# A recurrence and a token mixer as one hand-ordered program: another order of its steps, another queue for the last store

## The chip, the cores and the metric

The kernel runs on one core of a Trainium2 chip. The metric is device time in microseconds (us), given as the median of some runs. Five engines work from their own instruction lists: TensorE (PE, matmuls), VectorE (DVE), ScalarE (ACT), GpSimd (POOL) and SyncE (SP), which here issues nearly all the DMA transfers. An engine runs its list in the order in which it is written, and an instruction that waits for another engine holds up all that stand behind it.

## The reference

```python
f = sigmoid(f_logit)                                   # B=4, H=8, S=768, D=48
for t in range(S):                                     # first part: a gated recurrence
    state = f[:, :, t, :, None] * state + k[:, :, t] (outer) v[:, :, t]
    y[:, :, t] = q[:, :, t] @ state
x = y as (B, S, H * D)                                 # 4 x 768 x 384
theta = x @ w_theta                                    # second part
zr, zi = x * cos(theta), x * sin(theta)
u = x + w_tok_r @ zr + w_tok_i @ zi                    # mixes the 768 tokens
out = u + relu(u @ w_ch)                               # mixes the 384 channels
```

All inputs and the output are fp32.

## The kernel before

The recurrence runs in chunks of 128 tokens, 24 of them (4 batches of 6), each in two halves of 64. The second part runs per chunk up to the rotated z, and then in 8 groups (batch and half of the output tokens).

The program is one flat list of 1166 two-letter steps, `ORDER` (L53 to L89). Each letter pair is a function (L554 to L568), called with a running number of its own: the ninth `th` is chunk 8's angles. A suffix `/A`, `/D` or `/P` runs that step on ScalarE, VectorE or GpSimd in place of its usual engine; an `h` in front means one half of chunk 0. Every engine's list is the steps in this order (`manual_schedule`, L517), so the string alone sets who is ahead of whom on every engine and in the queues of transfers. The steps that matter below:

- **Loads** by SP: `lf`, `lk`, `lq` (a chunk's gate, k and q, 256 KB; L524), `lv` (v, 288 KB; L529), `lw` (a part of a weight, two transfers of 384 KB, tile `raw`; L178).
- **Gate:** `go` (exponential and logarithm, ScalarE, L237), `gs` (a running sum, VectorE, L242), `ge` (two exponentials, ScalarE: tiles `p` and `f`, L249), `gp` (copy of the last column of `p`, GpSimd, L253), `gq` (q times p, L257; on GpSimd with `/P`), `gk` (k times f, L262).
- **Recurrence of chunk m:** `ke` (transposes k, TensorE, L321), `kt` (copies them out, `ktok`, of which there is one buffer), `sc` (scores: v with ktok, L295, and q with k, L301), `sa`, `st`, `sm` (VectorE: middle state L330, new state L336, its fade L340, this one sometimes on GpSimd), `ma` (mask, L307), `oa` and `ob` (q with the states, L354; v with the masked scores, L365), `xc` (the copy of the result out of PSUM, tile `x`, L372), `xt` (transposes, L377), `xs` (a copy that is kept, tile `ut`).
- **Second part:** `xh`, `xl` (splitting x into two parts), `th` (angles, L407), `tn`, `se`, `ab` (the angle brought into range: L412, L418, L423), `tr` (two sines on ScalarE, L430, with a table load when the table changes), `ro` (z, L438), `zh`, `zl` (splitting z), `f` (a piece of the token products, L461, six matmuls; 144 pieces), `v`, `uh`, `ul` (u and its split), `c` (channel product, L479), `cv` (relu and sum, L493), `so` (a store, L500).
- **Weights:** `d2` (ScalarE reads the upper halves, L193, tile `top`), `d3` (VectorE joins the bits, L197), `d4`, `d5`, `e4`, `e5` (the split into two parts, L207 to L216).
- `wu` is a matmul whose result nobody reads (L316). `fl` and `rv` test whether the gates stayed in range; where they didn't, a slow path behind `tc.If` (L626) does all of it again.

Two pools of PSUM set much of the pacing. Bank "a" (4 buffers) holds scores, transposes and angles; "mix" (4) holds the products. Scores take two "a" banks per chunk, which are given back when `xc` has copied the result out. The last group's three stores go on ScalarE's queue: two in `store` (L499) and the third behind the slow path (L658).

Of the kernel before, what the change touches and what calls it, by code (L numbers as in the profile page):

```python
# [20 lines left out]
B, H, S, D = 4, 8, 768, 48  # L21
DM = H * D
P = 128
# [5 lines left out]
TH = 384  # L29
# [59 lines left out]
)  # L89


@with_exitstack
def gla_moe_kernel(
    ctx: ExitStack,
    tc: tile.TileContext,
    q: bass.AP,
    k: bass.AP,
    f: bass.AP,
    v: bass.AP,
# [605 lines left out]
```

## Time and profile before

| | us |
|---|---|
| median of 3 runs | 334.79 (334.3 to 336.13) |
| the profiled execution | 333.83 |
| its span, first to last instruction | 332.0 |
| TensorE busy | 319.2 (96%) |
| VectorE busy | 249.0 (75%) |
| ScalarE busy | 198.1 (60%) |
| GpSimd busy | 49.3 (15%) |

TensorE's granted clock is 0.999 of full speed over the span. The shares are means over very different stages, so the rows below give them by stretch. In the rows, L12 is line 12 of the kernel, `out<-in` are tiles by their names in the program, x is a count, and `ACTq` or `SPq` is the engine's list where it issues transfers. In chains and waits a name like "ACT x L146" stands for the instruction that was waited for.

### The profile page before, as it was taken

To read this page: it belongs to the slowest core of one execution; us is meant where nothing else is said; L and a number is where in the kernel's file an instruction comes from. 1 tells how busy PE (TensorE), PEld (TensorE's weight loads), DVE (VectorE), ACT (ScalarE), POOL (GpSimd) and SP (SyncE) were. 2 spreads that over 40 slices of the span, in tenths; PEclk is the share of its full clock that TensorE was granted. 3 is DMA by queue.
4 is the path that set the end of the run, shared out by engine and by line. 5 is a ranking of instruction groups with operands and counts; after the bars stand their busy time and mean duration, and the time that the engine had idled before them with its cause. 6 is when DMAs were issued, how large, how long until landed. Compare 5 with 4: busy or idle time off the path is not lost.

```text
span 332.0 us, 10297 instructions
## 1 busy us (share of the span) xinstructions
PE 319.2 (96%) x4430; PEld 295.3 (89%) x4430; DVE 249.0 (75%) x451; ACT 198.1 (60%) x361; POOL 49.3 (15%) x65
## 2 busy tenths in 40 slices
PE   7689999999998999999999999999999999999994
PEld 7578777668998999999999999999999999999993
DVE  3799999999997999898954686766687868533252
ACT  6789999995988978474765487526854024300000
POOL 3411123114234220012100220200010100000000
PEclk9999999999999999999999999999999999999999
DMA  7989998456543170253035134108101000000022
GB/s 213 351 264 318 348 328 325 143 190 251 193 148 101 36 232 36 67 190 115 24 113 196 43 129 138 57 2 265 46 2 38 28 24 26 0 24 26 24 73 76
DMA packets 22080, 43.16 MB, mean 130 GB/s; under 512 B 2448, under 2 KB 6288, under 8 KB 22032
## 3 DMA queue, kind: packets, MB, share of 16 engines
q1 hardware_dynamic: 21600, 41.88, 38.0%
q8 instruction: 36, 0.59, 0.7%
q10 hardware_dynamic: 432, 0.59, 0.5%
q14 instruction: 12, 0.10, 0.1%
HBM read 37.74 MB, written 4.72 MB: 128 GB/s over the span
## 4 chain that ended last, share of the span: by engine, by line
PE 85%; DVE 4%; DMA 4%; ACT 3%; SPq 1%; issue 1%; DVEq 0%; ACTq 0%
PE pm L461 43%; PE pch L479 12%; PE pth L407 11%; PE pss L365 4%; PE pss L354 4%; PE pss L295 3%; PE pss L301 3%; PE psk L321 3%; PE pxt L377 2%; DMA raw<-in_w_theta_dram 2%; DMA raw<-in_w_i_dram 2%; SPq L524 1%; DVE k L262 1%; ACT z L146 1%; ACT top L193 1%
## 5 line engine op out<-in xcount | busy, mean ns | idle before, releaser
L461 PE MATMUL pm<-wp,z 128*128 128x384 f32 x756 | 144.4, 340 | 0.0
L461 PEld LDWEIGHTS pm<-wp,z 128*128 128x128 f32 x756 | 130.1, 188 | 1.2 <-DVE wp L216 0.3
L479 PE MATMUL pch<-uhl,wch 128*128 128x384 f32 x216 | 41.4, 340 | 0.0
L479 PEld LDWEIGHTS pch<-uhl,wch 128*128 128x128 f32 x216 | 37.2, 188 | 0.2
L242 DVE TENSOR_TENSOR_SCAN f<-carry,f 128x512 f32<-128x512 f32 (+1 forms) x25 | 29.2, 1173 | 4.0 <-ACT f L238 3.9
L407 PE MATMUL pth<-wth,xh 128*128 128x384 f32 x144 | 30.1, 344 | 0.9 <-ACT x L146 0.9
L146 ACT CAST uhl<-ut 128x384 fp32r<-128x384 f32 x12 | 6.2, 516 | 38.0 <-DVE uhl L146 19.9
L493 DVE SCALAR_TENSOR_TENSOR ut<-pch,ut 128x384 f32<-128x384 f32 x24 | 13.1, 553 | 20.6 <-PE pch L479 20.6
L407 PEld LDWEIGHTS pth<-wth,xh 128*128 128x128 f32 x144 | 24.7, 188 | 1.7 <-ACT x L146 1.2
L461 PE MATMUL pm<-value,zf 128*128 128x384 f32 x72 | 26.0, 497 | 0.0
L307 DVE TENSOR_TENSOR sc<-pss,causal 128x256 f32<-128x256 f32 x48 | 18.0, 415 | 7.3 <-PE pss L354 7.1
L257 POOL TENSOR_TENSOR q<-q,p 128x512 f32<-128x512 f32 x13 | 17.2, 1323 | 41.0 <-ACT p L249 39.3
L340 POOL TENSOR_TENSOR st<-st,pes 128x192 f32<-128x192 f32 x12 | 8.7, 721 | 94.0 <-DVE st L336 94.0
L249 ACT ACTIVATE p<-f 128x512 f32<-128x512 f32 (+1 forms) x25 | 15.2, 609 | 9.8 <-DVE f L242 9.0
L253 POOL COPY pes<-p 128x4 f32<-128x4 f32 x24 | 11.4, 475 | 64.9 <-ACT p L249 64.9
L438 DVE TENSOR_TENSOR w<-w,x 128x768 f32<-128x768 f32 x18 | 17.4, 967 | 3.0 <-ACT w L431 2.9
L262 DVE SCALAR_TENSOR_TENSOR k<-f,k 128x512 f32<-128x512 f32 (+1 forms) x25 | 18.4, 740 | 1.2 <-ACT f L250 1.2
L146 ACT COPY x<-pss 128x192 f32<-128x192 f32 x34 | 9.1, 318 | 17.2 <-PE pss L365 17.1
L461 PEld LDWEIGHTS pm<-value,zf 128*128 128x128 f32 x72 | 12.8, 189 | 7.0 <-DVE zf L438 0.4
L365 PEld LDWEIGHTS pss<-v,sc 64*64 64x64 f32 x768 | 15.9, 134 | 3.1 <-issue 0.8
L365 PE MATMUL pss<-v,sc 64*64 64x48 f32 x768 | 18.4, 222 | 0.0
L295 PE MATMUL pss<-v,ktok 64*64 64x48 f32 x704 | 16.4, 220 | 1.7 <-DMA v<-in_v_dram 1.2
(86 smaller groups left out, 573.3 us busy)
## 6 DMA issues: line engine op xcount, KB each, us to landing
v<-in_v_dram SPq DMA_DIRECT2D x24, 288.0 KB, 3.8
f<-in_f_dram SPq DMA_DIRECT2D x23, 256.0 KB, 3.7
k<-in_k_dram SPq DMA_DIRECT2D x23, 256.0 KB, 4.1
q<-in_q_dram SPq DMA_DIRECT2D x23, 256.0 KB, 4.1
raw<-in_w_r_dram SPq DMA_DIRECT2D x12, 383.8 KB, 5.1
raw<-in_w_i_dram SPq DMA_DIRECT2D x12, 383.8 KB, 5.7
out_dram<-ut SPq DMA_DIRECT2D x21, 192.0 KB, 2.4
raw<-in_w_theta_dram SPq DMA_DIRECT2D x3, 383.8 KB, 6.3
```

The lines of the kernel that those rows point to most:

```text
L146: (nc.scalar.copy if on(usual) is nc.scalar else on(usual).tensor_copy)(dst, src)
L242: nc.vector.tensor_tensor_scan(fl, carry[:, pairs(h)].rearrange("p n t -> p (n t)"), fl, 0.0, ALU.mult, ALU.add)
L249: nc.scalar.activation(ps_[m][:, pairs(h)], ft, AF.Exp, scale=-1.0)
L257: on(nc.vector).tensor_tensor(qt, qt, ps_[m][:, pairs(h)], op=ALU.mult)
L262: nc.vector.scalar_tensor_tensor(kt, loaded["f", m][:, pairs(h)], E_TOP, kt, op0=ALU.min, op1=ALU.mult)
L295: nc.tensor.matmul(pkvs[m][t][r, p, :], kts[m][ts, p, r], vs[m][ts, h * D:(h + 1) * D], start=True, stop=True)
L307: masked = nc.vector.tensor_tensor(scs[m][j], pss[m][j][:, :, :64], causal.unsqueeze(1).to_broadcast([P, NP, 64]), op=ALU.mult)
L365: nc.tensor.matmul(pys[m][j][ts, p, :], l, r, start=(old[t] is None and p == 0), stop=(p == NP - 1))
L407: nc.tensor.matmul(pths[m], l, r, start=(n == 0), stop=(n == len(ms) - 1))
L438: nc.vector.tensor_tensor(zfs[m] if full else w, w, xs[m].unsqueeze(1).to_broadcast([P, 2, DM]), op=ALU.mult)
L461: nc.tensor.matmul(pms[g, d], l, r, start=(s == 0 and i == 0), stop=(s == NC - 1 and i == len(ms) - 1))
L479: nc.tensor.matmul(pcs[g, d], l, r, start=(es[0] == 0 and n == 0), stop=(es[-1] == KD - 1 and n == len(ms) - 1))
```

## The change

Three edits, of which the first is nearly all:

1. `ORDER` is replaced by another order of the same steps. The running numbers keep their meaning; what changes is where a step stands, and on which engine some of them run. Of the steps with a choice of engine, VectorE gets fewer `tn` (11 to 4) and `kt` (9 to 7), more `uh` (12 to 16), `xh` and `xc` (7 to 9 each); GpSimd gets chunk 0's `gq` halves and two more `d5`; ScalarE has 24 table loads where it had 26.
2. Chunk 0's q is loaded whole: one transfer of 256 KB, not two of 128 KB.
3. The last store goes through `store` to SP's queue, ahead of the slow path's branch; the line behind the slow path is gone. SP gets a branch hint as the other engines have.

```diff
 ORDER = (
-    "wu wu wu wu wu hlf hlq wu hlf hgo lf hgo lf hlq hlk hlk hgs hgs wu go hge hge go lk wu wu wu lw wu wu",
+    "wu wu hlf hlf wu hgo hgo hgs hlq hgs lf hge hge wu wu lf hgq/P hlk wu hgk wu wu hlk lw lk wu wu hgk lv",
...
-    "uh so so c ul cv v uh cv c bh rv ul f so cv so v uh/D ul c c c cv so cv so so cv",
+    "so cv so f f fl f f f ul f c v v c uh/D bh rv ul c uh/D cv so ul c cv so cv so cv so",
 )
...
     def store(b, g, d):
         th = g % NTH
-        queue = nc.scalar if g == B * NTH - 1 and not general else nc.sync
+        queue = nc.scalar if g == B * NTH - 1 and d < 2 and not general else nc.sync
         queue.dma_start(out[b, d * P:(d + 1) * P, th * TH:(th + 1) * TH], uts[g][:, d, :])
...
     fn = {"h" + s: lambda n, go=go: go(n // 2, n % 2) for s, go in by_halves.items()}
+    fn["hlq"] = by_halves["lq"]
...
-    fn["bh"] = lambda _: tc.mark_branch_hint_location("general", engines=[nc.tensor.engine, nc.vector.engine, nc.scalar.engine])
+    fn["bh"] = lambda _: tc.mark_branch_hint_location("general", engines=[nc.tensor.engine, nc.vector.engine, nc.scalar.engine, nc.sync.engine])
...
-    nc.scalar.dma_start(out[B - 1, 2 * P:, (NTH - 1) * TH:], uts[LAST][:, 2, :])
```

What the string moves shows best on the engines' own lists, at the places where TensorE waits. The number behind a letter is the chunk or part, the one behind `_` only a tile's serial number, and it differs between the two programs.

SP's transfers at the start, before (`raw0` is the first part of w_theta, `raw1` its rest):

```order
L524 DMA f0_102<-in_f_dram 128x256
L524 DMA q0_104<-in_q_dram 128x256
L524 DMA f0_102<-in_f_dram 128x256
L524 DMA f1_111<-in_f_dram 128x512
L524 DMA f2_115<-in_f_dram 128x512
L524 DMA q0_104<-in_q_dram 128x256
L524 DMA k0_118<-in_k_dram 128x256 x2
L524 DMA k1_133<-in_k_dram 128x512
L178 DMA raw0_138<-in_w_theta_dram 128x1535 x2
L524 DMA q1_155<-in_q_dram 128x512
L529 DMA v0_157<-in_v_dram 128x576
L529 DMA v1_164<-in_v_dram 128x576
```

and after:

```order
L701 BRANCH_PREFETCH_HINT
L524 DMA f0_99<-in_f_dram 128x256 x2
L524 DMA q0_109<-in_q_dram 128x512
L524 DMA f1_112<-in_f_dram 128x512
L524 DMA f2_121<-in_f_dram 128x512
L524 DMA k0_124<-in_k_dram 128x256 x2
L178 DMA raw0_131<-in_w_theta_dram 128x1535 x2
L524 DMA k1_134<-in_k_dram 128x512
L529 DMA v0_139<-in_v_dram 128x576
L524 DMA q1_142<-in_q_dram 128x512
L529 DMA v1_153<-in_v_dram 128x576
L524 DMA q2_172<-in_q_dram 128x512
```

The hint is new at the head, q0 is one row, w_theta stands ahead of k1, and v0 ahead of q1.

VectorE's list at the start, before, from the running sum of chunk 2 to chunk 1's new state:

```order
L242 SCALAR_TENSOR_TENSOR f2_115<-carry_67,f2_115 128x512
L262 SCALAR_TENSOR_TENSOR k1_133<-f1_111,k1_133 128x512
L197 SCALAR_TENSOR_TENSOR raw0_138<-raw0_138,top0_88 128x768
L330 COPY mid0_233<-pss00_199 128x192
L336 TENSOR_TENSOR st0_269<-pss01_200,mid0_233 128x192
L340 TENSOR_TENSOR st0_269<-st0_269,pes_82 128x192
L332 TENSOR_TENSOR mid1_280<-pss10_235,st0_269 128x192
L336 TENSOR_TENSOR st1_282<-pss11_236,mid1_280 128x192
```

and after:

```order
L242 SCALAR_TENSOR_TENSOR f2_121<-carry_67,f2_121 128x512
L262 SCALAR_TENSOR_TENSOR k1_134<-f1_112,k1_134 128x512
L197 SCALAR_TENSOR_TENSOR raw0_131<-raw0_131,top0_88 128x768
L257 TENSOR_TENSOR q1_142<-q1_142,p1_166 128x512
L330 COPY mid0_242<-pss00_198 128x192
L336 TENSOR_TENSOR st0_244<-pss01_199,mid0_242 128x192
L340 TENSOR_TENSOR st0_244<-st0_244,pes_82 128x192
L332 TENSOR_TENSOR mid1_282<-pss10_248,st0_244 128x192
L336 TENSOR_TENSOR st1_284<-pss11_249,mid1_282 128x192
```

The multiplication of q1 (L257), GpSimd's before, now stands here between the joining of w_theta's bits (L197) and chunk 0's middle state (L330).

ScalarE's list between the copy of chunk 10's keys and that of chunk 9's result, before:

```order
L146 COPY ktok10_1630<-psk10_1587 128x512
L430 ACT_TABLE_LOAD
L430 ACTIVATE w6_1340<-w6_1340 128x384
L431 ACTIVATE w6_1340<-w6_1340,pair_79 128x384
L430 ACTIVATE w7_1566<-w7_1566 128x384
L431 ACTIVATE w7_1566<-w7_1566,pair_79 128x384
L146 CAST z6_1693<-w6_1340 128x768
L146 CAST wp14_1695<-value4_731 128x768
L146 CAST wch1_87<-raw15_1580 128x384
L146 COPY x9_1723<-pss90_1438 128x4x48
L146 COPY x9_1723<-pss91_1439 128x4x48
```

and after:

```order
L146 COPY ktok10_1600<-psk10_1567 128x512
L146 COPY ut2_1205<-pxt8_1544 128x3x128
L146 CAST wch1_87<-raw14_1428 128x768
L193 CAST top0_88<-raw15_1558 128x384
L225 ACT_TABLE_LOAD
L249 ACTIVATE p12_1687<-f12_1310 128x512
L250 ACTIVATE f12_1310<-f12_1310 128x512
L146 CAST wp12_1707<-value2_408 128x768
L146 COPY x9_1717<-pss90_1436 128x4x48
L146 COPY x9_1717<-pss91_1437 128x4x48
```

The sines of w6 and w7 and the split of z6 (L146, `z6`) no longer stand between them; the gate of chunk 12 (L249, L250) with its table does.

TensorE's list at the angles of chunk 8, before:

```order
L461 MATMUL pm12_1363<-wp113_1523,z5_1574 128x384
L461 MATMUL pm12_1363<-wp013_1606,z5_1574 128x384
L461 MATMUL pm12_1363<-wp113_1523,z5_1574 128x384 x2
L461 MATMUL pm12_1363<-wp013_1606,z5_1574 128x384
L461 MATMUL pm12_1363<-wp113_1523,z5_1574 128x384
L407 MATMUL pth8_1749<-wth1_85,xh8_1584 128x384 x3
L407 MATMUL pth8_1749<-wth0_84,xh8_1584 128x384 x3
L407 MATMUL pth8_1749<-wth1_85,xl8_1624 128x384 x3
```

and after:

```order
L461 MATMUL pm11_1347<-wp113_1525,z5_1575 128x384
L461 MATMUL pm11_1347<-wp013_1614,z5_1575 128x384
L461 MATMUL pm11_1347<-wp113_1525,z5_1575 128x384 x2
L461 MATMUL pm11_1347<-wp013_1614,z5_1575 128x384
L461 MATMUL pm11_1347<-wp113_1525,z5_1575 128x384
L321 MATMUL psk11_1723<-ident_74,k11_1224 128x128 x4
L407 MATMUL pth8_1730<-wth1_85,xh8_1625 128x384 x3
L407 MATMUL pth8_1730<-wth0_84,xh8_1625 128x384 x3
L407 MATMUL pth8_1730<-wth1_85,xl8_1679 128x384 x3
```

One product piece that stood ahead of the angles has moved away (`pm12`, behind this place now), and the transposes of k11 stand ahead of them.

## Rows read from the trace of the kernel before

**Rows 1.** busy us of each engine by stretch (x instructions), granted clock, DMA share, GB/s

```profile
16.00:33.00 17.00, 15.07 (x382) 13.47 (x375) 16.43 (x31) 15.78 (x34) 3.20 (x4) 1.00 0.88 285
33.00:72.00 39.00, 39.00 (x631) 28.06 (x630) 38.13 (x66) 37.66 (x68) 7.76 (x9) 1.00 0.76 270
72.00:107.00 35.00, 34.10 (x510) 31.18 (x508) 33.03 (x53) 28.05 (x51) 13.59 (x10) 1.00 0.56 180
107.00:327.00 220.00, 219.76 (x2755) 212.28 (x2755) 152.03 (x287) 105.32 (x188) 19.20 (x27) 1.00 0.23 74
```

**Rows 2.** TensorE's waits: engine, line, waited for, us in total, times, longest

```profile
PE pss L295 <- DMA v<-in_v_dram: 1.2, 1, 1.2
PE pth L407 <- ACT x L146: 0.9, 1, 0.9
PE pss L295 <- ACT ktok L146: 0.5, 2, 0.3
```

**Rows 3.** the chain of waits, first 36 us: start us, us, what

```profile
5.53 6.68 DMA raw<-in_w_theta_dram
...
13.43 1.62 DVE raw L197
...
15.89 1.47 DVE st L340
...
17.46 0.37 DVE mid L332
...
34.26 2.05 PE pm L461 x6
```

**Rows 4.** timeline of ScalarE: start, us, instruction, [idle before <- releaser]

```profile
14.55 0.59 ACT L146 COPY ktok<-psk 128x512 f32<-128x512 f32 x1 [1.21 <-PE pss L295]
```

**Rows 5.** timeline of ScalarE, 84 to 110 us

```profile
88.45 0.52 ACT L146 COPY x<-pss 128x192 f32<-128x192 f32 x2
...
91.77 0.49 ACT L412 ACTIVATE w<-pth 128x384 f32<-128x384 f32 x1 [1.08 <-PE pth L407]
93.14 0.48 ACT L146 CAST xh<-pxt 128x384 fp32r<-128x384 f32 x1 [0.89 <-PE pxt L377]
...
104.95 0.84 ACT L146 CAST z<-w 128x768 fp32r<-128x768 f32 x1 [1.43 <-DVE w L438]
...
106.86 0.53 ACT L146 COPY x<-pss 128x192 f32<-128x192 f32 x2
```

**Rows 6.** timeline of TensorE, 100 to 110 us

```profile
102.22 0.78 PE L365 MATMUL pss<-v,sc 64*64 64x48 f32 x32
...
107.22 1.32 PE L407 MATMUL pth<-wth,xh 128*128 128x384 f32 x6 [0.90 <-ACT x L146]
```

**Rows 7.** timeline of GpSimd, 0 to 62 us

```profile
15.87 1.27 POOL L257 TENSOR_TENSOR q<-q,p 128x512 f32<-128x512 f32 x1
...
43.39 1.26 POOL L340 TENSOR_TENSOR st<-st,pes 128x192 f32<-128x192 f32 x1 [4.06 <-DVE st L336]
```

**Rows 8.** timeline of VectorE, 9 to 34 us

```profile
29.51 0.35 DVE L340 TENSOR_TENSOR st<-st,pes 128x192 f32<-128x192 f32 x1
...
32.24 0.95 DVE L197 SCALAR_TENSOR_TENSOR value<-raw,top 128x768 int32<-128x768 int32 x1
```

**Rows 9.** timeline of VectorE, the last 7 us

```profile
326.14 1.60 DVE L493 SCALAR_TENSOR_TENSOR ut<-pch,ut 128x384 f32<-128x384 f32 x3 [2.09 <-PE pch L479]
```

**Rows 10.** the output's stores from 327 to 328.3 us: ns min/median/max, starts, landing

```profile
L500 ACTq DMA_DIRECT2D out_dram<-ut x2: 386/706/1027, 326.7 to 327.2; - x2
...
DMA to landing us min/median/max: 2.5/2.7/3.0
```

**Rows 11.** the output's stores from 328.5 to 330 us

```profile
L658 ACTq DMA_DIRECT2D out_dram<-ut x1: 432/432/432, 328.7 to 328.7; - x1
...
DMA to landing us min/median/max: 2.0/2.0/2.0
```

**Rows 12.** the page's DMA issues: count, KB each, median us to landing

```profile
out_dram<-ut SPq DMA_DIRECT2D x21, 192.0 KB, 2.4
```

66 rows, old and new, of the table ORDER are left out of this document.

## The prediction

> **What bounds the kernel now.** I read the stretches first, because a share over the whole span mixes stages. In [rows 1] the reader is to see four stages. From 16 to 33 us ScalarE is busy for 15.78 of 17 us and VectorE for 16.43 of 17, while TensorE has holes. From 33 to 72 us TensorE is busy for all 39.00 us, and VectorE (38.13) and ScalarE (37.66) run almost as full beside it. From 72 to 107 TensorE has its only larger hole after the start. From 107 to 327 us TensorE is busy for 219.76 of 220 us with the other engines far below it. So from about 34 us on the span is TensorE's own work, and that work is the same 1166 steps before and after, less one transfer. An order can gain in three places only: before 34 us, in the hole near 106 us, and behind TensorE's last matmul at 327 us.
>
> The list of TensorE's waits comes next [rows 2]: 1.2 us for chunk 0's v, 0.9 us before an angle product (L407) for the copy of x, and 0.5 us for ktok. Then the chain of waits of the first 34 us [rows 3] shows what the start hangs on: the transfer of w_theta (issued 5.53, landed 12.21), its joining on VectorE (13.43, 1.62 us), the fade of chunk 0's state (15.89, 1.47 us), chunk 1's middle state (17.46), and at last the first product, f0, at 34.26.
>
> **The head.** The new order of SP's transfers sends k1 behind w_theta and q1 behind v0. Each is 256 KB. With the transfers at 0.88 of their time the next stretch moved 285 GB/s [rows 1]; at that rate 256 KB are 0.9 us, and I count 0.7, since several transfers share the queue. So w_theta lands near 11.5 us and v0 about 0.7 us sooner too, which is inside the 1.2 us that the first scores wait for v [rows 2]. What pays for it is k1, which lands near 12; VectorE's step on k1 stands ahead of the joining of w_theta, and its end at about 12.7 us is still level with ScalarE's conversion that the joining needs. q1 is now VectorE's, behind the joining, and takes a slot there that GpSimd had.
>
> The joining itself took 1.62 us beside a GpSimd multiplication of q; the same operation on the same shape takes 0.95 us alone [rows 3, 7, 8]. GpSimd's q1 is gone from that moment (its q0 halves are early), so −0.67. The fade took 1.47 us beside GpSimd's q2 (15.87 to 17.14) against 0.35 us alone [rows 3, 7, 8]. In the new order q2 needs an exponential that now stands behind a 0.9 us conversion of w_theta on ScalarE, so the fade at about 15.5 us is over before q2 starts near 16: −1.1. Against these stands q1 on VectorE, +0.7 at most, beside the wait for the scores.
>
> Walking the new order with these durations, chunk 0's scores start at about 13.1 instead of 13.8, ktok of chunk 1 near 13.9 instead of 14.55 [rows 4], and chunk 1's middle state near 15.9 instead of 17.46: the chain leads by 0.7 to 1.6 us. It can't all arrive: from 16 us ScalarE has only 17 − 15.78 = 1.22 us of idle time up to the first sines [rows 1], and in the new order the conversions of w_theta and chunk 3's gate stand ahead of x0. Bounds for f0: 0 (ScalarE eats all) and −1.6. I take **−0.9**: the 0.7 us with which ktok leads, and a little of ScalarE's slack. Loading q0 whole costs nothing there, since it is read only after chunk 0's exponentials.
>
> **The hole at 106 us.** [Rows 6] show the angle product of chunk 8 starting at 107.22, after 0.90 us of nothing. It waits for a PSUM bank: the "a" banks are four, and the one it needs is emptied by the copy of x9 on ScalarE. That copy ran at 106.86 behind z6, wp14 and wch1, and z6 had made ScalarE wait 1.43 us for VectorE [rows 5]; the attention matmuls that x9 reads were done at 103.0 [rows 6].
>
> In the new order I count ScalarE's rows from x8 to x9: by the durations of this trace they are about 17.2 us before and 15.8 after (out go tn7, xh8, z6 and wp14, all with their waits; in come w6's and w7's absolute values, z5 and the gate of chunk 12). Before, x8 ran at 88.45 and x9 18.41 us later, of which 1.08 + 0.89 + 1.43 = 3.40 us were waits for work that is no longer there [rows 5]. So x9 comes 18.41 − 3.40 − 1.4 = 13.6 us after x8. x8 itself can't be earlier than TensorE gives it: the attention of chunk 8 now stands one product piece (f23, about 1 us) further back, at 89.5: x9 near 103.1, or at once after the attention of chunk 9 at about 104. TensorE wants the bank after f34, now for the transposes of k11, one product piece earlier than before and so near 105.0. The cover is about half a us once x9 is copied; the two pairs of sines in front are what can use it up. I take **−1.0**: the 0.90 us and a tenth, since matmuls overlap at their ends. Its bounds are −1.1 and, if ScalarE is as late as it is today while TensorE wants the bank one piece earlier, +0.9.
>
> **The rest between 34 and 327 us.** ScalarE has two table loads less and VectorE some 4 us less work, GpSimd about 4 us more; under a full TensorE that is worth nothing. The two waits for ktok make 0.5 us together [rows 2]. The new order puts about 3.4 us more of ScalarE's work ahead of ktok9 and only 1.0 us more of TensorE's, so that one stays, and I allow for two more of its size and for SP's added branch hint: **+0.4**. Bounds: −0.7 (all of [rows 2]'s ktok waits and the 0.24 us of 107 to 327 go) and the rival below.
>
> **The tail.** VectorE's last operation ends at 327.74 [rows 9]. Before, the last of three stores was issued only behind the branch, at 328.7, and landed 2.0 us later, at 330.7 [rows 11]. The two ahead of it were issued at 326.7 and 327.2 and landed after up to 3.0 us, so at 330.2 [rows 10]. Now SP issues the last one at about 327.8, and SP's stores land after 2.4 us [rows 12]: 330.2 as well. So **−0.5**, no more, because the second store is late next. Bounds 0 (the end waits for something else) and −0.9 (the 328.7 to 327.8 in full).
>
> **Sum.** −0.9 − 1.0 + 0.4 − 0.5 = −2.0. The profiled execution took 333.83 us (span 332.0 and 1.83 around it): 331.8. The median of the runs, 334.79, lies 0.96 above that execution, so I predict 332.8. About 0.5%, 1.7 us, is what a measurement of this kernel tells from no change.
>
> **Rivals.**
> *The gains come back as other waits.* A lead at 34 us is kept only if no operand is late after it, and VectorE and ScalarE are within 1 or 2 us of full up to 72 us [rows 1]. If they eat the head's lead and the hole at 106 moves to another bank or ktok, only the tail is left: 333.83 − 0.5 + 0.96 = 334.3. For it: every wait of TensorE here has a ScalarE or VectorE copy behind it. Against it: VectorE's load falls.
>
> *GpSimd holds up VectorE between 33 and 72 us (slower).* The new order hands GpSimd q4, q6 and the fade of chunk 2 in or before this stretch. Where the two engines met, each lost: GpSimd's fade of chunk 4 took 1.26 us, as long as its q, VectorE's joining and fade lost 0.67 and 1.1 [rows 3, 7, 8]. If each of GpSimd's three stops VectorE for its whole length, that is 3 × 1.27 = 3.8 us. VectorE has 39 − 38.13 = 0.87 us to spare, so it decides from there, and the head's lead goes too: −1.0 − 0.5 + 0.4 + 3.8 = +2.7, or 337.5 us. Against it: q operations of this kind stood in that stretch before too, and TensorE was full beside them.
> The Trainium skill, "SBUF — State Buffer", section "SBUF: two separate sides", says that GpSimd and a VectorE operation with two SBUF inputs take a shared pair of ports as an exclusive lock, the loser waiting for the whole instruction. The 1.47 against 0.35 us agree. By that rule GpSimd's work is never free beside a full VectorE, and the sum would be this rival's; by the full TensorE of [rows 1] it would be mine.
>
> *Everything goes.* The head keeps its whole 1.6, no hole re-forms, both ktok waits go: −1.6 − 1.1 − 0.7 − 0.5 = −3.9, or 330.9 us. It needs ScalarE to give up all its slack in the head.
>
> *The fetch of TensorE's instructions, which the change speaks of, does nothing.* In 220 us from 107 on TensorE is idle for 0.24 us [rows 1]; there is next to nothing that a better placed fetch could return. That is part of my forecast already.
>
> **How the numbers follow.** Forecast 0.50 (its own range 331.4 to 334.2; two thirds of it under 333.1, where faster begins), other waits 0.25 (no change), everything goes 0.12 (faster), GpSimd 0.13 (nearly all slower). Faster: 0.33 + 0.12 = 0.45; same: 0.17 + 0.25 + 0.01 = 0.43; slower 0.12. The range reaches from the best case with a little spread, 330.0, into GpSimd's, 336.6.
>
> **What would show it.** Right: the joining of w_theta and the first fade at 0.95 and 0.35 us, f0 at 33.4 or earlier, no wait for x before L407 near 105, a store by SP at 327.8 less the gains, and nothing of ScalarE's queue after it. Wrong: TensorE under 38 of 39 us from 33 to 72, VectorE operations there of 1.3 us and more beside GpSimd's q, or a wait over 0.5 us for ktok9 or x9.

## The result: slower by 0.7%, and the profile after

The changed kernel took 338.05 us (median of 20 runs, 335.25 to 340.0), the kernel before 335.51 us beside it (20 runs, 332.96 to 340.41). The ratio is 1.007, with a 95% interval of 1.0052 to 1.0089: slower by some 2.35 us. The forecast of 332.8 us had the wrong sign, and the time lies above its range. The profiled execution took 336.98 us with a span of 335.3 us, against 333.83 and 332.0.

TensorE's timeline splits that difference into three:

| us | before | after | difference |
|---|---|---|---|
| first product, f0, starts | 34.11 | 35.31 | +1.20 |
| from there to the end of TensorE's last matmul | 293.03 | 294.86 | +1.83 |
| from there to the end of the span | 4.87 | 5.09 | +0.22 |

The sum, 3.25 us, is that of two single executions. The kernel before was lucky in its own: in five runs with the old start f0 began at 34.1 to 36.4 us, 35.3 on average. So +1.20 is not what the start costs; the experiments settle it.

The stretches after (busy us of TensorE, its weight load, VectorE, ScalarE and GpSimd, each with its instructions, then the granted clock, the share of the DMA engines and GB/s), which answer to [rows 1]:

```profile
16.00:33.00 17.00, 14.43 (x326) 12.86 (x330) 13.70 (x27) 13.78 (x31) 4.61 (x7) 0.90 0.75 256
33.00:72.00 39.00, 38.15 (x650) 27.65 (x643) 36.44 (x62) 37.47 (x63) 11.61 (x11) 1.00 0.74 249
72.00:107.00 35.00, 35.00 (x510) 31.42 (x509) 33.06 (x54) 30.14 (x56) 11.55 (x9) 1.00 0.51 173
107.00:330.00 223.00, 221.76 (x2765) 213.53 (x2763) 154.75 (x291) 101.77 (x185) 23.11 (x27) 1.00 0.26 79
```

The hole between 72 and 107 us is gone (35.00 of 35.00). In its place TensorE idles for 0.85 us in the stretch before and for 1.24 us in the one behind, where it had idled for 0 and 0.24. GpSimd works more in both (11.61 for 7.76, 23.11 for 19.20). From 16 to 33 us VectorE and ScalarE, which were full, are 2 to 3 us emptier, and the granted clock is 0.90 for 1.00.

TensorE's waits after (line, waited for, us in total, times, longest) answer to [rows 2]:

```profile
PE psk L321 <- DVE k L262: 2.4, 2, 1.6
...
PE pss L354 <- issue: 1.7, 1, 1.7
PE pss L365 <- DVE sc L307: 0.7, 1, 0.7
...
PE pth L407 <- DVE w L418: 0.4, 1, 0.4
PE psk L321 <- DVE ut L146: 0.3, 1, 0.3
PE pm L461 <- DVE zf L438: 0.3, 1, 0.3
```

None of the three waits of [rows 2] is left. Of the six shown here the first, for k, stood in the kernel before too (1.7 us in all); the other five are new. The chain of waits after (start us, us, what), for [rows 3]:

```profile
15.48 0.37 DVE st L336
...
15.89 0.56 PE pss L354 x23
16.45 1.74 issue
18.18 0.27 PE pss L354 x4
...
35.47 0.65 PE pm L461 x2
```

VectorE's timeline from 12 us, for the joining and the fade of [rows 3, 8]:

```profile
12.05 0.96 DVE L197 SCALAR_TENSOR_TENSOR raw<-raw,top 128x768 int32<-128x768 int32 x1 [0.40 <-ACT top L193]
...
14.44 0.36 DVE L340 TENSOR_TENSOR st<-st,pes 128x192 f32<-128x192 f32 x1
```

Both steps of the head came out as forecast, at 0.96 and 0.36 us, and chunk 1's middle state stood at 15.02 for 17.46. In the midst of chunk 0's attention products, whose states were there, TensorE then stopped for 1.74 us. "Issue" says that it waited for nothing that the profile shows. The cause is one row further, in the DMA queues between 15.5 and 16 us (packets, MB, share):

```profile
q8 instruction: 1, 0.02, 12.1%
```

That is one packet of 16 KB of instructions. It began at 15.71 us, and TensorE went on 2.5 us later, with its 222nd matmul. The kernel before, in the same half microsecond:

```profile
q8 instruction: 1, 0.02, 13.0%
```

There the packet began at 15.67, but the operands of that matmul came only at 18.3 us: chunk 0's scores had waited 1.2 us for v, and the fade of chunk 0 ended at 17.36. So no stop could show. It does show in three of the other four profiles with the old start (runs of the next section), whose scores came up to 1.4 us sooner and whose fade was as slow (1.47 us): at the same 222nd matmul TensorE stands for 0.93 us in e2, 0.38 in e4 and 1.22 in e7. TensorE's wait in e7:

```profile
PE pss L354 <- issue: 1.2, 1, 1.2
```

In the changed kernel, behind the stop the granted clock was 0.57 from 19 to 23 us, between the two levels (1.2 and 2.4 GHz); it had been 1.00 from 16 to 19.

### The profile page after: what moved, and what is told of

Same layout as the page of the kernel before. It is cut to its first block, busy times and chain, and to the rows that moved or that the text cites. A ratio compares the mean times of both kernels' runs of the same rounds, so it can differ in the third digit from the quotient of the medians.

```text
span 335.3 us, 10303 instructions
## 1 busy us (share of the span) xinstructions
PE 321.2 (96%) x4430; PEld 296.1 (88%) x4430; DVE 247.9 (74%) x449; ACT 195.8 (58%) x357; POOL 56.4 (17%) x69
## 3 DMA queue, kind: packets, MB, share of 16 engines
HBM read 37.74 MB, written 4.72 MB: 127 GB/s over the span
## 4 chain that ended last, share of the span: by engine, by line
PE 77%; DVE 8%; DMA 6%; issue 3%; SPq 2%; ACT 2%; DVEq 0%; ACTq 0%
PE pm L461 40%; PE pch L479 10%; PE pth L407 9%; PE pss L365 4%; PE pss L354 3%; DMA k<-in_k_dram 3%; PE pss L295 3%; PE pss L301 3%; PE psk L321 2%; DMA raw<-in_w_i_dram 2%; PE pxt L377 2%; DVE k L262 1%; SPq L524 1%; DMA out_dram<-ut 1%; PE warm L316 1%
## 5 line engine op out<-in xcount | busy, mean ns | idle before, releaser
L242 DVE TENSOR_TENSOR_SCAN f<-carry,f 128x512 f32<-128x512 f32 (+1 forms) x25 | 32.6, 1308 | 2.6 <-ACT f L238 2.6
L257 POOL TENSOR_TENSOR q<-q,p 128x512 f32<-128x512 f32 (+1 forms) x15 | 21.8, 1455 | 33.9 <-DMA q<-in_q_dram 8.9
L412 ACT ACTIVATE w<-pth 128x384 f32<-128x384 f32 x20 | 9.8, 488 | 26.6 <-PE pth L407 23.2
L249 ACT ACTIVATE p<-f 128x512 f32<-128x512 f32 (+1 forms) x25 | 15.4, 616 | 13.5 <-DVE q L257 10.3
L445 DVE TENSOR_TENSOR z<-w,z 128x768 fp32r<-128x768 f32 x18 | 17.0, 951 | 6.5 <-ACT z L146 6.4
L253 POOL COPY pes<-p 128x4 f32<-128x4 f32 x24 | 8.4, 348 | 78.6 <-ACT p L249 78.6
L465 DVE TENSOR_TENSOR ut<-pm,ut 128x384 f32<-128x384 f32 x24 | 13.2, 549 | 10.2 <-PE pm L461 10.2
```

The lines of the kernel that those rows point to most:

```text
L242: nc.vector.tensor_tensor_scan(fl, carry[:, pairs(h)].rearrange("p n t -> p (n t)"), fl, 0.0, ALU.mult, ALU.add)
L249: nc.scalar.activation(ps_[m][:, pairs(h)], ft, AF.Exp, scale=-1.0)
L257: on(nc.vector).tensor_tensor(qt, qt, ps_[m][:, pairs(h)], op=ALU.mult)
L445: nc.vector.tensor_tensor(zs[m][:, 0], zfs.get(m, ws.get(m)), zs[m][:, 1], op=ALU.subtract)
L465: nc.vector.tensor_tensor(u, pms[g, d], u, op=ALU.add)
```

## The experiments

Eleven runs are compared with the kernel before, timed beside them on the same chip; two (e8, e9) are single executions. "Rest" is the time from f0's start to the end of the last matmul.

### Which part costs the time

The order is cut at the first product: one kernel has the old steps up to f0 and the new ones behind it (e2), one the other way round (e3), and one only the last store (e4). e2 and e3 have the new store too.

```diff
 old start, new rest:  ORDER = steps_before[:first f] + the other steps as the changed order has them
 new start, old rest:  ORDER = steps_after[:first f]  + the other steps as the order before has them
 store alone:          ORDER as before, with a last "so";  queue = ... and d < 2 ...;  SP's hint;  L658 away
```

> All steps up to the first product as in the kernel before, the rest in the changed order, last store on SP. Theory 1 (the loss is made in the start, and the waits after 36 us follow from a start that is late): first product at 34.1, the new waits between 36 and 72 us (0.6 us at 60.6, 0.46 at 68.6) gone, time 1 us below the kernel before. Rival (the new order of the rest loses by itself, some 2 us of new waits against 1.5 won back at 86 and 106): time 0.5 to 1 us above the kernel before.

Measured: 338.56 us, ratio 1.0125 (1.0078 to 1.0172); rest 294.89 us. The new rest loses by itself. As a whole e2 is 2.6 to 5.8 us slower than the kernel before, more than its rest explains (1.9 us longer); where the difference comes from is open.

> All steps up to the first product in the changed order, the rest as in the kernel before, last store on SP. Theory 1: the hole at 16.45, the halved clock behind it and a first product near 35.3 are all there, and the time is 1 to 2 us above the kernel before. Rival (the start costs nothing in the end, because what follows has slack for 1.2 us): time as the kernel before, within 0.5 us.

Measured: 335.46 us, ratio 1.0017 (0.9989 to 1.0045); rest 292.90 us. The stop is there (1.44 us at 16.59), and the clock of 0.57 from 19 to 23 us, and f0 starts at 35.21; yet the kernel takes the time of the one before.

> The kernel before with the third edit alone: the last store by SP, ahead of the branch. By the prediction the end comes 0.5 us sooner. Theory now (two stores issued at once by two engines slow each other: ScalarE's second takes 1.5 us to issue where it took 1.0, and lands last): from TensorE's last matmul to the end 5.1 us where the kernel before has 4.9, so the time within 0.3 us of the kernel before, rather longer.

Measured: 336.17 us, ratio 1.0014 (0.9992 to 1.0035). From the last matmul to the end its profile shows 5.59 us, for 4.87 before: no gain from SP's store. That profile is of the slowest of its 13 executions, so the ratio tells more.

So the start is worth about nothing, the store nothing (the two ratios allow for −0.4 to +1.5 and −0.3 to +1.2 us), and the rest some 1.9 us. Over all runs the rest is 292.75 to 293.03 us with the old order behind f0 (seven runs) and 294.59 to 295.26 with the new one (six). Not counted are e5, below, which changes the new order there, and the store alone, whose profiled execution took 339.41 us, 3.2 over its own median, with a rest of 297.08 us and a granted clock of 0.57 from 80 to 84 us.

### The stop at 16.5 us

Is it the packet of instructions, and what does the packet wait for?

```diff
 e1, in the changed order (v2 ahead of the weight part raw2):
-... wu ke kt d3 lw lv sc
+... wu ke kt d3 lv lw sc
```

> The changed kernel, with the first token weight (raw2, two transfers of 384 KB) one place later in SP's list, behind v2, which waits for chunk 0's attention; so 768 KB less stand in the DMA queues from 12.5 to 19 us. Theory 1 (the 1.74 us hole in TensorE at 16.45 is the fetch of its own next instructions, which stands behind SP's transfers): the 16 KB instruction packet starts at 14.5 us or sooner instead of 15.7, the hole is under 0.7 us, TensorE's clock stays at 1.0 through 16 to 33 us, the first product starts at 33.5 or sooner instead of 35.3, and the time falls by 1.5 to 3 us. Rival (the packet is asked for at a fixed place of TensorE's list and comes when it comes, transfers or not): packet at 15.7, hole 1.7 us, first product at 35.3, time the same or up to 1 us longer since raw2 is late.

Measured: 338.71 us, ratio 1.0118 (1.0084 to 1.0152). The packet still began at 15.9 us, against the theory, and the DMA engines were still busy for 0.90 of the time from 15 to 16 us. The stop was only 0.35 us, because TensorE itself came later (its 81st matmul at 13.99 us, for 12.75 in the changed kernel). So this run doesn't tell the theory from its rival.

```diff
 e8, in the changed order (five loads behind v2):
-lq lw lf lf gk d2 lk wu ke kt d3 lw lv
+lq gk d2 wu ke kt d3 lv lw lf lf lk lw
```

> The changed kernel with five loads of the start (the rest of w_theta, the gates of chunks 3 and 4, k of chunk 2, the first token weight) all behind v2 in SP's list, so that nothing is issued between 9 and some 18 us; its time is not of interest. Theory 1a (TensorE's next 16 KB of instructions stand behind SP's transfers): the packet that starts at 15.7 in all kernels so far starts at 14.5 or sooner, and TensorE goes on at its 222nd matmul by 17 us. Rival 1b (the packet comes at its own time): 15.4 to 15.9, and the 222nd matmul at 18.0 to 18.5 us as before.

One execution, 343.44 us. With the loads held back the packet began at 13.9 us, between 13 and 14.5 us, when the queues were nearly empty:

```profile
q8 instruction: 1, 0.02, 4.0%
```

and the chain of waits of this kernel (start us, us, what) has no stop:

```profile
16.00 0.37 DVE st L336
...
16.41 0.62 PE pss L354 x27
```

All attention products run through where the changed kernel stopped after 23. TensorE was no further along than there (its 81st matmul at 12.98 us, for 12.75), yet the packet came 1.8 us sooner, so the rival of a packet that comes at its own time falls. That the kernel as a whole is slower is the price of the late loads: f0 at 41.98.

```diff
 e9, in the changed order (seven idle matmuls moved behind the second ob):
-... go gs go gs wu wu wu wu wu ge wu kt lq ... lk wu ke ... ma ob ma ob go
+... go gs go gs ge kt lq ... lk ke ... ma ob ma ob wu wu wu wu wu wu wu go
```

> The changed kernel with the seven filler matmuls (14 passes, 28 instructions with their weight loads) between the first two transposes of k moved behind chunk 1's attention. If TensorE stops where the instructions that it holds end, it stops 14 passes later in the work: not inside the 32 passes of L354 at the 23rd, but at the 5th of L365, again until 18.0 to 18.5 us. Rival (that very L354 matmul waits for an operand that the profile doesn't name): it stops at the same matmul as before.

One execution, 340.82 us, and no answer: without those matmuls the granted clock was 0.51 from 13 to 20 us, TensorE was slow, the packet began only at 17.25, and no stop shows.

The stop can be removed by smaller means, if q3 is asked for earlier, so that SP's list waits ahead of f4 for the buffer that q3 needs.

```diff
 e10, new start and old rest; e11, the changed order:
-lq lw lf lf gk d2 lk wu ke kt d3 lw lv sc
+lq lw lf lq lf gk d2 lk wu ke kt d3 lw lv sc
 e12, the order before:  lk ke kt ... lv wu lq xh   ->   lq lk ke kt ... lv wu xh
 e14, as e10 with k2 ahead of the gate, and the last store as before:
-lq lw lf lf gk d2 lk wu ke
+lq lw lf lk lq lf gk d2 wu ke
```

> The changed order up to the first product and the old order after it, with one load moved: q3, which waits for chunk 0's attention, now stands in SP's list ahead of the gate of chunk 4, k of chunk 2 and the first token weight, so these 1.3 MB are issued near 15.5 us and not from 11.7. Theory 1 (TensorE's instruction packet stands behind SP's transfers, and TensorE goes on at its 222nd matmul some 2.5 us after the packet starts): packet at 14.0 to 14.6, 222nd matmul at 16.6 to 17.2, first product at 33.5 to 34.3, time 0.8 to 1.5 us below the kernel before. Rival (VectorE and ScalarE, or the late loads, eat the lead before the first product): first product at 35 or later, time as the kernel before or up to 0.5 us above.

> The changed kernel with the same one move of q3. Theory 1: packet and first product as in the run with the old rest, 1 to 1.5 us sooner than in the changed kernel; then the waits of the rest, which cost 1.8 us, bring the time to 0.2 to 0.4% above the kernel before. Rival: time as the changed kernel, 0.6 to 0.8% above the kernel before.

> The kernel before with q3 moved ahead of k2, f4, k3 and the first token weight in SP's list. Its own operands reach the 222nd matmul only at 17.6 to 18.7, so an earlier packet gives it little: packet at 14.5 or sooner, 222nd matmul at 17.5 to 18, first product at 34 to 34.5, time 0 to 0.7 us below the kernel before. Rival: the late loads (k2 after 20 us) make it 0.5 to 1.5 us slower.

> The changed order up to the first product and the old order behind it with the old last store, and in SP's list k of chunk 2 right behind the gate of chunk 3, then q3 (which waits for chunk 0's attention), then the gate of chunk 4 and the first token weight. Theory 1 (in the earlier run with q3 as a gate the lead at the 222nd matmul, 1.3 us, was lost to k of chunk 2 alone, which came 2 us late): packet at 14.5 to 15.2, 222nd matmul at 16.9 to 17.5, no wait for k of chunk 2 at 21 to 23 us, first product at 33.5 to 34.3, time 0.7 to 1.4 us below the kernel before. Rival (ScalarE and VectorE, which are full from 16 to 33 us, take the lead whatever is loaded when): first product at 35 or later, time as the kernel before within 0.4 us.

| | packet starts | 222nd matmul | f0 | rest | median us, ratio (95%) |
|---|---|---|---|---|---|
| e10 | 14.5 | 16.92 | 36.10 | 292.75 | 335.91, 1.0019 (0.9983 to 1.0054) |
| e11 | 13.6 | 16.29 | 34.07 | 295.26 | 337.89, 1.0081 (1.0046 to 1.0117) |
| e12 | 14.4 | 17.41 | 34.59 | 292.85 | 336.16, 1.0032 (1.0004 to 1.006) |
| e14 | 14.4 | 16.98 | 34.12 | 292.88 | 335.29, 1.0000 (0.9968 to 1.0033) |

The packet starts, the 222nd matmuls and f0 are of one profiled execution each. The packet comes earlier in all four, and the 222nd matmul about where each theory has it; the times that the theories forecast, 0 to 1.5 us below the kernel before in e10, e12 and e14 and 0.2 to 0.4% above it in e11, did not come. e12 is even slower by some 1.1 us, as its rival has it. From 15 to 16 us the DMA engines are busy for 0 to 0.08 of the time in these four and e8, and for 0.87 or more in the ten other profiles. In e10 k2 paid for the gain. TensorE's waits of e10 from 14 to 37 us:

```profile
PE psk L321 <- DVE k L262: 1.9, 1, 1.9
```

e11 waits 1.58 us for k2 too and still starts f0 at 34.07, with a granted clock of 1.00 from 16 to 33 us; its new rest then loses as ever. e14 asks for k2 ahead of the gate. Its chain (start us, us, what):

```profile
16.06 0.56 PE pss L354 x23
16.62 0.35 issue
16.98 0.27 PE pss L354 x4
...
34.28 2.58 PE pm L461 x8
```

Of the stop 0.35 us is left, and f0 starts 1.1 us ahead of the new start's usual 35.2 to 35.5. The median doesn't show it: its interval reaches 1.1 us down, and in the profile the end took 5.97 us behind the last matmul. No version here beats the kernel before.

### The rest: who makes TensorE wait

```diff
 e5, in the changed order (two low parts of weights and one q from GpSimd to VectorE):
-... oa d5/P lk f ro d2        -... ma xh d5/P c v       -... v lq gq/P sa th
+... oa lk f ro d5 d2          +... ma xh d5 c v         +... v lq gq sa th
```

> The changed kernel with three of GpSimd's steps on VectorE: the split of wp08 (now behind the rotation of chunk 5), the split of wp04 and q times p of chunk 15, which ran at 65.4, 112.6 and 155.6 us beside a VectorE operation that took 0.7, 1.16 and 0.97 us longer than its like. Theory 2 (the new order puts GpSimd's long operations beside those of VectorE on which TensorE waits, and the two exclude each other): TensorE's waits at 68.6 (0.46 us), 115.1 (0.93) and 158.0 (0.51) fall under 0.2 us each, and the time falls by 1 to 1.9 us against the changed kernel, to 0.2 to 0.4% above the kernel before. Rival (the chains on VectorE are late for their length; 2.6 us more work on VectorE make them later): the three waits stay or grow, time as the changed kernel's or up to 1 us above.

Measured: 337.12 us, ratio 1.006 (1.0029 to 1.0092); rest 293.90. The three waits (zf at 68.6, the mask at 115, k at 158) are gone, and half of the lost 1.9 us with them. The median is 0.9 us below that of the changed kernel, but the ratios differ by only 0.001 (1.006 for 1.007), and their intervals overlap. What shows instead, TensorE's waits of e5 from 36 us on:

```profile
PE pss L295 <- issue: 1.1, 1, 1.1
PE pm L461 <- DVE ut L465: 0.5, 1, 0.5
PE pm L461 <- DVE ut L493: 0.3, 1, 0.3
```

The first looks like the instructions again: their next packet began between 36.6 and 36.8 us, and TensorE stopped amid 32 equal matmuls and went on at 39.04. The other two are at 120.25 and 122.45, 5 and 7 us behind the place of the mask. Ahead of them another meeting of the two engines stands in e5's timelines of VectorE and GpSimd:

```profile
113.26 0.34 DVE L146 CAST uhl<-ut 128x384 fp32r<-128x384 f32 x1
...
117.13 2.59 DVE L216 TENSOR_TENSOR wp<-value,wp 128x768 fp32r<-128x768 f32 x1
```

```profile
117.06 1.85 POOL L216 TENSOR_TENSOR wp<-value,wp 128x768 fp32r<-128x768 f32 x1 [8.21 <-ACT w L431]
```

VectorE's split of a weight took 2.59 us where the one at 111.19 took 0.94. The cast, with no GpSimd operation beside it, took 0.34.

```diff
 e7, in the order before (copy of x9 ahead of zh6, d4, e4):
-... ro d3 gp zh d4 gs ul e5/P ob e4 f xc ro
+... ro d3 gp gs ul e5/P ob f xc zh d4 e4 ro
```

> The kernel before, with only the copy of chunk 9's result (x9) put ahead of z6, wp14 and the second part of w_ch on ScalarE. The prediction's step on the hole at 106 us: the 0.9 us wait of TensorE before chunk 8's angles is gone, nothing takes its place, and the time falls by 0.9 to 1.1 us. Rival (the wait comes back at the next copy on ScalarE, since ScalarE is late there by itself): another wait of 0.7 us or more between 104 and 120 us, time as the kernel before.

Measured: 335.81 us, ratio 1.0012 (0.9977 to 1.0047); rest 293.03, to the hundredth that of before. The wait for x9 is gone; e7's TensorE at 114.73 (start us, us, instruction, [idle before <- releaser]):

```profile
114.73 0.25 PE L354 MATMUL pss<-st,q 48*64 48x48 f32 x1 [0.75 <-DVE st L336]
```

One edit that removes the hole gets a new one of nearly its size 7.5 us later (114.73 for 107.22), as in the changed kernel (115.06), but behind another step. Both wait for VectorE. For e7 that shows in its load. From 104 to 110, 110 to 116 and 116 to 122 us VectorE is busy for all 6.00 us in the kernel before and in e7 (in the changed kernel for 5.12, 6.00 and 6.00); e7's rows (columns as in the stretches above):

```profile
104.00:110.00 6.00, 6.00 (x102) 5.91 (x94) 6.00 (x9) 4.48 (x10) 1.71 (x1) 1.00 0.46 139
110.00:116.00 6.00, 5.25 (x97) 4.72 (x98) 6.00 (x13) 5.37 (x8) 1.44 (x2) 1.00 0.00 0
116.00:122.00 6.00, 5.93 (x111) 5.59 (x102) 6.00 (x12) 4.03 (x10) 2.19 (x1) 1.00 0.62 174
```

If VectorE's work sets the pace there, less of it should keep the gain. e13 is e7 without the low parts of two parts of the token weights (left out, not moved).

```diff
 def split_lo(n):
+    if n in (2, 3):
+        parts[n][2][0] = place(n, 1)
+        return
```

> The kernel before with x9 first on ScalarE (as in the run of that name), and without two splits of token weights (parts 2 and 3, one on GpSimd at 103.9 us, one on VectorE at 112.5; their low parts are left out and the high parts stand in for them in the products, so the matmuls are as many as before). Theory 3 (from 104 to 122 us VectorE is the limit, and a hole of TensorE that one order closes there opens again at VectorE's next result): no wait of TensorE over 0.4 us from 104 to 122 us, time 0.9 to 1.4 us below the kernel before. Rival (TensorE waits there for something else): a wait of 0.7 us or more remains, time as the kernel before.

Measured: 335.14 us, ratio 0.9966 (0.993 to 1.0002); rest 292.96. TensorE's stretches from 104 to 122 us (columns as above):

```profile
104.00:110.00 6.00, 6.00 (x68) 5.91 (x63) 6.00 (x9) 5.63 (x11) 0.05 (x1) 1.00 0.55 139
110.00:116.00 6.00, 6.00 (x163) 5.70 (x163) 5.04 (x13) 5.97 (x11) 1.70 (x3) 1.00 0.18 46
116.00:122.00 6.00, 5.72 (x62) 5.19 (x62) 6.00 (x9) 2.90 (x8) 1.66 (x1) 1.00 0.65 197
```

TensorE idles for 0.28 us in these 18 us, for 0.81 in e7 and 0.91 before, so with less work on VectorE the hole doesn't come back at its size. But small waits grew elsewhere (85 to 88 us), the rest is as long as ever, and the interval touches 1: it leans to VectorE as the limit and doesn't settle what the stretch is worth.

## Why the prediction was wrong, step by step

**The head, −0.9: failed.** The transfers, the joining (0.96) and the fade (0.36) came as worked out. The chain led not by 0.7 to 1.6 us but by 2.44 (15.02 for 17.46), and then it stood. The step that failed is "Bounds for f0: 0 (ScalarE eats all) and −1.6": ScalarE is not what ate it: its load fell from 15.78 to 13.78 us. What ate the lead was the fetch, the rival that I set aside by the stretch from 107 us on. At the 222nd matmul 0.51 us of the lead is left (18.18 for 18.69). The place to look was the first 20 us, where transfers fill the queues ([rows 1], share 0.88) and TensorE was to arrive sooner. In the profile of the kernel before the late packet was covered by the late scores and the slow fade. That no wait of before showed it is the lesson of this term: I took the wait that ended last for the only one.

The Trainium skill, "Runtime: NRT & Kernel Launch", section "Instruction fetch mechanics", says that a sequencer fetches its own 16 KB blocks ahead and that crossing into the next one is mostly hidden. The profile of the kernel before agrees; the changed kernel, with its 1.74 us, and e2, e4 and e7 with their 0.38 to 1.22 don't. By that rule the head would have kept its lead.

Is the lost lead itself a loss? The ratio 1.0017 of the new start with the old rest says no, within −0.4 to +1.5 us. The profile that I had flattered the old start: in the other four f0 began at 35.0 to 36.4 us, with a granted clock of 0.90 from 16 to 33 us in each, for 34.11 and 1.00. The clock is the other part of it: from the 222nd matmul to f0 that profile took 15.4 us, and the ten with 0.90 (e10, held up by k2, apart) took 16.8 to 17.5, with either start. So the packet sets the 222nd matmul with either start, unless its operands come later still. What follows goes with the clock; no run varies the clock alone. The term is about 0 where −0.9 stood.

**The hole at 106 us, −1.0: right at its place, worth nothing.** x9 was copied at 106.65, ahead of the transposes of k11 at 107.49, and TensorE is full from 72 to 107. (x9 was not as early as I had it, 103.1 to 104: ScalarE waited 1.60 us for GpSimd's q at 104.73.) The sum's step that failed is "−1.0: the 0.90 us and a tenth": I didn't ask what is late next. It is the mask of the next chunk, on VectorE (why it was late there stands under the next term); TensorE's timeline after:

```profile
107.49 0.60 PE L321 MATMUL psk<-ident,k 128*128 128x128 f32 x4
...
115.06 0.94 PE L365 MATMUL pss<-v,sc 64*64 64x48 f32 x30 [0.73 <-DVE sc L307]
```

e7 shows such an exchange in the old order, with an unchanged rest. For this term the rival that the gains come back as other waits was the right one.

**The rest, +0.4: failed, and the largest miss.** Together with the hole it measured +1.9 us, where −0.6 stood. The step that failed is "GpSimd about 4 us more; under a full TensorE that is worth nothing". The removed waits, the hole among them, gave back about 1.5; new ones of 0.3 to 0.9 us stand at 49.7, 55.2, 60.6, 68.6, 80.5, 115, 158 and 239 us by the spacing of TensorE's matmuls, some too short for the list of waits. Three of them I followed, and each has VectorE on one side and GpSimd on the other. VectorE after, three places:

```profile
66.95 1.64 DVE L438 TENSOR_TENSOR zf<-w,x 128x768 f32<-128x768 f32 x1
...
113.16 1.51 DVE L146 CAST uhl<-ut 128x384 fp32r<-128x384 f32 x1
114.59 0.74 DVE L307 TENSOR_TENSOR sc<-pss,causal 128x256 f32<-128x256 f32 x2
...
155.76 1.65 DVE L262 SCALAR_TENSOR_TENSOR k<-f,k 128x512 f32<-128x512 f32 x1
...
157.80 0.34 DVE L146 CAST uhl<-ut 128x384 fp32r<-128x384 f32 x1
```

and GpSimd after, the same three:

```profile
65.36 2.42 POOL L216 TENSOR_TENSOR wp<-raw,wp 128x768 fp32r<-128x768 f32 x1 [7.31 <-ACT wp L146]
...
112.55 1.90 POOL L216 TENSOR_TENSOR wp<-value,wp 128x768 fp32r<-128x768 f32 x1 [3.80 <-ACT wp L146]
...
155.56 1.29 POOL L257 TENSOR_TENSOR q<-q,p 128x512 f32<-128x512 f32 x1 [5.61 <-DMA q<-in_q_dram]
```

The reader is to add start and time on each pair. GpSimd's first ends at 67.78, and zf ends 0.81 us later, after 1.64 us for the 0.95 it took in the kernel before; GpSimd's second ends at 114.45, and the cast, 0.34 us when alone, ends 0.22 later; the third ends at 156.85, and k, 0.69 us at 10.96, ends 0.56 later. VectorE got on when GpSimd was done, each time, and the mask, the products or the transposes behind it came late. In e5, without GpSimd beside them, the same cast took 0.34 us (at 113.26) and the same zf 0.95 (at 67.42), and the waits were gone. GpSimd worked 7.1 us more in all (56.4 for 49.3) where I had counted 4, and VectorE only 1.1 less (247.9 for 249.0) where I had counted 4.

So the rival "GpSimd holds up VectorE" had the mechanism, with 0.13 for its chance. That its 337.5 us is close to the 338.05 measured is luck: its 3.8 us were 1.9 in the three waits (0.46, 0.93 and 0.51), and the −1.0 and −0.5 in its sum did not come. Its place was right for one of the three only: I had it from 33 to 72 us, and with q and the fade. It acted at 65, 113 and 156 us, and twice in the split of a weight. e5 takes the three meetings away and gets half of the 1.9 us back in the rest; new in it are a stop of 1.1 us at the next packet and waits of 0.5 and 0.3 us behind a further meeting at 117 us. The waits at the other places were not taken apart, so their cause is open.

The rule of the Trainium skill that I weighed, "SBUF — State Buffer", section "SBUF: two separate sides", is borne out with its detail that the lock holds against VectorE operations with two SBUF inputs: at 66.04 a middle state, with one input in PSUM, took 0.33 us beside the same GpSimd split that held zf. The cast has one input, from SBUF; the section also counts operations in a two-port mode, and whether this is one no run shows.

**The tail, −0.5: failed.** SP issued its store at 330.82 (VectorE's last operation ran from 329.16 for 1.60 us), as worked out. The step that failed is "so at 330.2": the second store, which I had as next in line, landed later than before (ScalarE's two took 3.0 and 3.5 us). The output's stores after (ns min/median/max, starts; then landing):

```profile
L500 ACTq DMA_DIRECT2D out_dram<-ut x2: 388/946/1504, 329.8 to 330.3; - x2
L500 SPq DMA_DIRECT2D out_dram<-ut x1: 332/332/332, 330.8 to 330.8; - x1
...
DMA to landing us min/median/max: 2.5/3.0/3.5
```

Against [rows 10, 11] the issue of the second took up to 1.50 us for 1.03, and the slowest landed after 3.5 for 3.0. In ten profiles with SP's store the end came 4.86 to 5.59 us behind the last matmul, 5.15 on average; in five with ScalarE's it was 4.72 to 5.97, 5.10 on average (4.87 in the median, against 5.15). There is no gain in it.

**The sum by the runs:** start 0, hole and rest +1.9, tail +0.1 (5.15 for 5.10; +0.3 by the medians): +2.0 us, for the 2.35 measured, whose interval reaches from 1.7 to 3.0.

## What to carry to other kernels

When a lead is won at the start, look at TensorE's instruction packets in the DMA queues: where its operands come earlier than the packet, the lead ends there, and the profile before can hide it behind a wait that ended a moment later. When a hole of a full pipeline is closed, ask what is late next in the stretch behind it: two different edits closed the same hole and got another 7.5 to 8 us on, in e7 with VectorE full for 18 us, in the changed kernel behind a cast that GpSimd held up. Work handed to GpSimd is to be priced by the VectorE operations beside it (here those with two SBUF operands, and a cast), and by what is queued behind them.

## What the runs showed of the hardware that was not expected

- The packet of 16 KB with TensorE's next instructions goes behind data: it began at 15.4 to 15.9 us in eight profiles with the DMA engines full, at 16.9 and 17.3 us in two more (e7, e9), and at 13.6 to 14.5 us where loads were held back (e8, e10, e11, e12, e14). TensorE went on 2.4 to 2.7 us after the packet began in all nine profiles in which it stopped there, with either start at its 222nd matmul, and 2.2 to 2.4 us after the next packet in e5. That the packet is TensorE's own is read from this timing; no row names its engine.
- After the stop of 1.74 us the granted clock was 0.57 over 4 us; in e11, without a stop at that place, it was 1.00 from 16 to 33 us, though TensorE waited 1.58 us for k2 at 21.5 us. But it was 0.90 from 16 to 33 us in e12 and e13 too, which had no stop there: what makes it fall is not shown.
- A cast of 128x384 with one input, 0.34 us alone, took 1.51 us beside a GpSimd operation.
- Three stores on two queues ended 5.15 us behind the last matmul on average, three on one queue 5.10.
